# One row scale per chunk from norms, half-array products first, and first loads on two queues

## The chip, the cores and the metric

The kernel runs on one core of one Trainium2 chip. A core has five engines that run their own instruction lists in order and wait for each other by semaphores: TensorE (PE, with its weight loads shown as PEld), VectorE (DVE), ScalarE (ACT), GpSimd (POOL) and SyncE (SP), which here only issues DMAs. The metric is the device time of one execution in microseconds. Three timed runs of the kernel before took 1389.17, 1389.33 and 1389.57 us, so the median is 1389.33 us. All positions in time below are microseconds from the start of the span of the one profiled execution.

## What is computed

Cut to what matters, with B = 8, S = 4160, D = 192, H = 8 heads, K = 7 taps, and 33280 rows in all:

```
w   = softmax(weight_gen, axis=-1)              # per row and head, over 7 taps
y   = sum_k w[..., k, h] * x_pad[row + k]       # causal window of 7 rows of x
h   = y @ w_in                                  # 192 -> 1024
sm  = exp(h - max(h)) / (sum(exp(h - max(h))) + 1e-9)
s   = h * sm                                    # "solu"
ln  = (s - mean(s)) / sqrt(var(s) + 1e-6) * g_ln
out = ln @ w_out                                # 1024 -> 192
```

The output is normalised over each row of s, so a factor common to a row of s drops out again, except in the two small constants. The kernel uses this: it multiplies s by a scale of its own choice that keeps the 16-bit halves of s in range.

## The kernel before

The 33280 rows lie as 128 runs of 260 rows, one run on each partition, so a tile is one row of every run, 128 rows in all, and there are 260 tiles. x and weight_gen come in chunks: of 4 tiles, of 8, and then fifteen of 16. Per chunk, seven steps (t0 to t6) make the softmax over the taps on DVE, POOL and ACT. For each group of four tiles (two in the first chunk) POOL runs three tensor operations (line 133 multiplies x by the taps, lines 139 and 141 add), and DVE adds the last two parts (line 366, the step `fin`).

A tile then passes through these steps. PE transposes it (`xT`, line 383, two tiles at a time), ACT copies a rounded part (`xhi`, line 391), the rest comes from PE and ACT (`xn` and `xlo`, lines 398 and 405) or from DVE (`xld`, line 412). PE makes h (`mm1`): 192 rows of w_in are 128 and 64, the 128 use the whole array (line 422, six matmuls) and the 64 use one half of the array for each half of h (line 427, six matmuls, two at a time). DVE takes the negative maximum of the row (`max`, line 441). It then makes a bound out of the maximum (`vb`, line 445) and its reciprocal (`vr`, line 450), the scale of the row. ACT makes the exponentials (`exp`, line 454), DVE the product h times scale times exponential (`solu`, line 460), ACT the squares (`sq`, line 466) and a 16-bit part (`hi`, line 473), DVE the remaining 16-bit part (`lo`, line 477). One DMA transposes both (`tr`, line 485), PE makes the second product out of 24 matmuls (`mm2`, line 529), and ACT scales it (`out`, line 540). The factors of the rows come out of eight small steps per four tiles (f0 to f7, lines 497 to 516). A store follows per four tiles.

At the start w_in and w_out, which arrive as 64-bit floats, are turned into 32-bit floats by DVE and ACT out of integer pieces (lines 194 to 213), in seven parts. h lies in three PSUM buffers, so `mm1` of a tile waits for `sq` and `lo` of the tile three before. `po`, which `mm2` writes, has one buffer, so `mm2` waits for `out` of the tile before.

The order of the work on every engine is written out ahead: `issue_order` runs a list of steps with a cost, an earliest time and the steps each waits for, and picks on every engine the step with the lowest key, its tile number plus an entry of the table `URGENCY`. Nothing moves at run time. All DMAs stand on SP's queue. The loads of chunk 0 and the weights stand in the code ahead of that order: the first taps, two loads of the last 64 rows of w_in, then in `load_x(0)` a load of the six rows ahead of each run (line 78, 127 rows of the tile `xt`), of the first rows (line 79) and of zeros (line 80), and behind them the rest of w_in, w_out, g and chunk 1 (lines 168 to 177).

Of the kernel before, what the change touches and what calls it, by code (L numbers as in the profile page):

```python
# [26 lines left out]
def tile_kernel(ctx: ExitStack, tc: tile.TileContext, x, weight_gen, w_in, w_out, g_ln, out):  # L27
# [39 lines left out]
    def load_x(c, part=0):  # L67
# [5 lines left out]
        if c == 0:  # L73

            nc.gpsimd.memset(xt[:1, : HALO * D], 0.0)
            zeros = const.tile([B, D], F32, name="zeros")
            nc.gpsimd.memset(zeros, 0.0)
            nc.sync.dma_start(xv[1:, :HALO, :], x_run[: P - 1, RUN - HALO :, :])
            nc.sync.dma_start(xv[:, HALO : HALO + n, :], x_run[:, :n, :])
# [49 lines left out]

    def attention(xt, wt, t, n, half):  # L130
# [54 lines left out]
    def float_of_double(key, raw, n, step):  # L185
# [17 lines left out]
        elif step == 2:  # L203

            frac = big.tile([P, FF], F32, name="e")[:, :n]
# [18 lines left out]
    def last_rows(step):  # L224
        if step < 3:
            first["b"] = float_of_double("b", raw_b, FH, step)
        elif step == 3:
            nc.scalar.copy(wb_hi, first["b"])
        elif step == 4:
            nc.vector.tensor_tensor(  # L230
                out=wb_lo, in0=first["b"], in1=wb_hi.bitcast(F32), op=ALU.subtract
            )

# [26 lines left out]
    def scale_and_sum(f, step):  # L260
# [17 lines left out]
        elif step == 2:  # L278
            junk = big.tile([P, FF], F32, name="e")
# [5 lines left out]
    def prepare_second(step, half=None):  # L285
# [8 lines left out]
        elif step == 5:  # L294
            second["total"] = ps_a.tile([P, 512], F32, name="pa")
            nc.tensor.matmul(second["total"][:, :NP], ones, sq, start=True, stop=True)
# [119 lines left out]
    def first_product(t):  # L416
# [3 lines left out]
        for fs in halves:  # L420
            for n, (lhs, rhs) in enumerate(((hi, wa_hi), (hi, wa_lo), (lo, wa_hi))):
                nc.tensor.matmul(h[:, fs], lhs[:, 0, :], rhs[:, fs], start=n == 0, stop=False)  # L422

        for n, (lhs, rhs) in enumerate(((hi, wb_hi), (hi, wb_lo), (lo, wb_hi))):
            for f, fs in enumerate(halves):
                rows = slice(f * D2, (f + 1) * D2)
                nc.tensor.matmul(  # L427
                    h[:, fs], lhs[rows, 1, :], rhs[rows], start=False, stop=n == 2,
                )
# [12 lines left out]


    def bound(t):
        nc.vector.tensor_reduce(
            stat(t, BOUND), stat(t, NMAX, 2), axis=AX.X, op=ALU.max, apply_absolute_value=True
        )

    def row_scale(t):
        nc.vector.reciprocal(stat(t, SIGMA), stat(t, BOUND))  # L450
# [38 lines left out]
    def scales(t, step):  # L489
# [9 lines left out]
        if step == 0:  # L499
            nc.scalar.activation(of(ZE), of(Z), AF.Copy, bias=1e-9)  # L500
        elif step == 1:
            reduce(U, ZE, 2, ALU.mult)
        elif step == 2:
            nc.scalar.activation(of(E), of(U), AF.Square, scale=1e-3 * FF**1.5)
        elif step == 3:
            reduce(V, Q, 2, ALU.add)
        elif step == 4:
# [5 lines left out]
        elif step == 5:  # L513
            reduce(T, Y, 3, ALU.mult)
        elif step == 6:
# [3 lines left out]
        elif step == 7:  # L519
            reduce(OUT, Y2, 2, ALU.mult)  # L520
# [30 lines left out]
    def at_chunk(op, *args):  # L551
# [5 lines left out]
        max=maximum, vb=bound, vr=row_scale, exp=exponentials, solu=solu, sq=squares, hi=high_half, lo=low_half,  # L557
# [18 lines left out]
    for n in range(8):  # L576
        ops[f"f{n}"] = at(scales, n)
    for n in range(TAP_STEPS):
        ops[f"t{n}"] = at_chunk(softmax_taps, n)
# [9 lines left out]
    a00=-79.4, a01=-110.4, a02=-10.4, a03=-9.5, a04=28.3, a10=35.2, a11=8.2, a12=-10.4, a13=2,  # L589
    a14=-26.4, attA=14.7, attB=-118.7, b0=12.5, b1=28.4, b2=-7.8, b3=-40.9, b4=125.7, c00=120.1,  # L590
    c01=19.2, c02=4.8, c10=-143, c11=7.6, c12=1.7, c20=-15.4, c21=6.6, c22=-4.8, c30=-11.2,
    c31=-125.2, c32=78.7, dup=-17.9, exp=66.3, f0=73.9, f1=1.2, f2=-140.6, f3=-73.6, f4=-146.4,
    f5=-90.9, f6=-122.6, f7=-80.2, fin=-1.8, hi=21.6, lo=-147.6, lw=-22, lx0=-1.4, lx1=-11.2,
    lx2=-124.2, lx3=169.4, max=5.1, mm1=26.4, mm2=33.4, od=-130.9, out=-6, p30=-16.2, p31=3.9,
    p4=42.9, p5=103.1, p6=5.8, p70=-62.9, p71=0.3, p80=126.7, p81=-54.7, q00=-14.5, q01=-183.5,
    q02=-5.9, q10=-13.7, q11=-25.1, q12=-13.9, q20=-2.5, q21=-143.1, q22=-168.3, q30=-15.9,
# [246 lines left out]
```

## Time and profile before

| what | value |
|---|---|
| median of three timed runs | 1389.33 us |
| profiled execution, own time | 1389.4 us |
| its span | 1387.5 us, 1.9 us less than its time |
| mean granted PE clock | 0.991 |
| PE busy | 1259.2 us (91%) |
| POOL busy | 1247.0 us (90%) |
| DVE busy | 1230.0 us (89%) |
| ACT busy | 1128.5 us (81%) |
| first `max` (line 441) starts | 60.1 us |
| last `max` starts | 1365.3 us |

Busy time is the union of an engine's instructions, so operations that overlap on one engine are counted once. A group of instructions is named by line, engine, operation and the tiles it writes and reads, with its count, busy time and mean duration; behind the bar stands how long the engine was idle just ahead of them, and what ended that idle time. SPq is a DMA being issued on SP's queue; "issue" as releaser is time in which nothing in the profile was waited for.

### The profile page before, as it was taken

How to read it: one execution, taken by the hardware profiler on the slowest of the kernel's cores; microseconds unless marked ns; L12 is line 12 of the kernel's file. 1: busy time of each engine (PE TensorE's matmuls, PEld its weight loads, DVE VectorE, ACT ScalarE, POOL GpSimd, SP SyncE). 2: the span in 40 equal slices, each digit the busy share in tenths (PEclk: the TensorE clock that was granted, in tenths of full speed). 3: DMA queues.
4: the chain of work that ended last, by engine and by line, in shares of the span. 5: the costliest groups of instructions: out<-in, count | busy, mean ns of one | idle time of the engine just before them, and what ended most of it. 6: DMA issues, size and time to landing. Idle time of an engine off the chain costs nothing.

```text
span 1387.5 us, 26562 instructions
## 1 busy us (share of the span) xinstructions
PE 1259.2 (91%) x10028; PEld 988.6 (71%) x10028; DVE 1230.0 (89%) x2068; ACT 1128.5 (81%) x2231; POOL 1247.0 (90%) x243
## 2 busy tenths in 40 slices
PE   0389899999999999989989999999999999999997
PEld 0267677777777777767767677777777777777776
DVE  2999898999989899889989898989899889999984
ACT  1588887888888888888888888888788888888885
POOL 1999999999999999999999999999999999999100
PEclk9989999999999999999999999999999999999999
DMA  3469768696968789697857768687858668766765
GB/s 90 139 142 194 147 128 201 124 207 122 194 130 174 146 145 195 122 198 123 186 130 166 158 149 186 118 190 145 193 109 191 146 140 176 132 133 117 134 131 116
DMA packets 565241, 210.43 MB, mean 152 GB/s; under 512 B 544329, under 2 KB 545785, under 8 KB 565112
## 3 DMA queue, kind: packets, MB, share of 16 engines
q1 hardware_dynamic: 565112, 208.73, 72.5%
q8 instruction: 79, 1.29, 0.4%
q14 instruction: 50, 0.41, 0.1%
HBM read 46.19 MB, written 25.56 MB: 52 GB/s over the span
## 4 chain that ended last, share of the span: by engine, by line
POOL 51%; DVE 16%; issue 13%; ACT 13%; PE 4%; DMA 3%; SPq 0%; POOLq 0%; DVEq 0%; ACTq 0%
POOL pr L133 27%; POOL pr L139 15%; POOL half L141 6%; DVE h L460 5%; ACT hl L473 4%; DVE hl L477 4%; ACT e L466 3%; DVE stats L441 3%; ACT e L454 3%; DVE a L366 3%; DMA xt<-in_x_dram 2%; POOL wt L114 2%; PE po L529 2%; POOL wt L126 1%; PE h L422 1%
## 5 line engine op out<-in xcount | busy, mean ns | idle before, releaser
L133 POOL TENSOR_TENSOR pr<-xt,wt 128x5376 f32<-128x5376 f32 (+1 forms) x66 | 631.3, 9565 | 23.1 <-DMA xt<-zeros 20.5
L529 PE MATMUL po<-w_hl,hlT 128*128 128x192 f16 x6192 | 558.5, 247 | 26.6 <-ACT ot L540 26.2
L529 PEld LDWEIGHTS <-hlT 128*128 128x128 f16 x6240 | 515.2, 98 | 82.2 <-issue 79.2
L477 DVE SCALAR_TENSOR_TENSOR hl<-h,hl 128x1024 f16<-128x1024 f32 x260 | 315.4, 1220 | 44.2 <-ACT e L466 31.5
L460 DVE SCALAR_TENSOR_TENSOR h<-h,stats,e 128x1024 f32<-128x1024 f32 x260 | 334.7, 1288 | 22.4 <-ACT e L454 9.2
L473 ACT ACTIVATE hl<-h 128x1024 f16<-128x1024 f32 x260 | 267.3, 1028 | 92.3 <-DVE stats L497 57.4
L139 POOL TENSOR_TENSOR pr<-pr 128x2304 f32<-128x2304 f32 (+1 forms) x66 | 332.7, 5041 | 5.2
L441 DVE TENSOR_REDUCE stats<-h 128x1 f32<-128x1024 f32 x260 | 316.1, 1216 | 8.9 <-PE h L427 8.1
L454 ACT ACTIVATE e<-h,stats 128x1024 f32<-128x1024 f32 x260 | 292.6, 1126 | 31.1 <-DVE stats L441 27.2
L466 ACT ACTIVATE e<-h,stats 128x1024 f32<-128x1024 f32 x260 | 292.3, 1125 | 5.9 <-DVE hl L477 5.4
L422 PE MATMUL h<-wa_hi,x_hi 128*128 128x512 f32 x520 | 225.4, 433 | 36.3 <-ACT e L466 22.8
L141 POOL TENSOR_TENSOR half<-pr 128x1536 f32<-128x1536 f32 (+1 forms) x66 | 225.8, 3422 | 5.2
L422 PE MATMUL h<-wa_hi,x_lo 128*128 128x512 f32 x520 | 207.5, 399 | 0.8 <-ACT x_lo L405 0.8
L422 PE MATMUL h<-wa_lo,x_hi 128*128 128x512 f32 x520 | 206.3, 397 | 0.0
L422 PEld LDWEIGHTS h<-wa_hi,x_hi 128*128 128x128 f32 x520 | 98.9, 190 | 59.3 <-ACT e L466 26.0
L427 PE MATMUL h<-wb_hi,x_hi 64*128 64x512 f32 x520 | 131.1, 500 | 0.0
L383 PE MATMUL pa<-ident,a 128*128 128x128 f32 x520 | 84.6, 286 | 44.2 <-DVE a L366 44.1
L540 ACT ACTIVATE ot<-po,stats 128x192 f32<-128x192 f32 x258 | 111.4, 432 | 8.5 <-PE po L529 8.5
L366 DVE TENSOR_REDUCE a<-half 128x768 f32<-128x1536 f32 (+1 forms) x66 | 116.4, 1764 | 1.6 <-POOL half L141 1.6
L427 PEld LDWEIGHTS h<-wb_hi,x_hi 64*128 64x128 f32 x520 | 48.6, 184 | 96.7 <-issue 96.7
L422 PEld LDWEIGHTS h<-wa_hi,x_lo 128*128 128x128 f32 x520 | 98.6, 190 | 24.3 <-ACT x_lo L405 1.6
L383 PEld LDWEIGHTS pa<-ident,a 128*128 128x128 f32 x520 | 55.8, 142 | 79.7 <-DVE a L366 44.1
(79 smaller groups left out, 1194.1 us busy)
## 6 DMA issues: line engine op xcount, KB each, us to landing
out_dram<-ot SPq DMA_DIRECT2D x65, 384.0 KB, 3.3
xt<-in_x_dram SPq DMA_DIRECT2D x30, 576.0 KB, 4.7
xt<-in_x_dram SPq DMA_DIRECT2D x30, 480.0 KB, 4.7
wt<-in_weight_gen_dram SPq DMA_DIRECT2D x15, 448.0 KB, 4.1
hlT<-hl SPq DMA_TRANSPOSE x260, 4.5
raw<-in_moe_w_out_dram SPq DMA_DIRECT2D x1, 1536.0 KB, 9.4
xt<-in_x_dram SPq DMA_DIRECT2D x3, 384.0 KB, 6.0
raw_a<-in_moe_w_in_dram SPq DMA_DIRECT2D x2, 512.0 KB, 11.5
```

The source lines that it names most:

```text
L133: nc.gpsimd.tensor_tensor(out=window(pr, 0, [(TG * D, K), (HG, n * H), (1, HG)]), in0=window(xt, t * D, [(D, K), (HG, n * H), (1, HG)]), i ...
L139: nc.gpsimd.tensor_tensor(out=pr[:, :3], in0=pr[:, :3], in1=pr[:, 3:6], op=ALU.add)
L141: nc.gpsimd.tensor_tensor(out=half, in0=window(pr, 0, [(2 * TG * D, 2), (D, n), (1, D)]), in1=window(pr, TG * D, [(5 * TG * D, 2), (D, n), ...
L422: nc.tensor.matmul(h[:, fs], lhs[:, 0, :], rhs[:, fs], start=n == 0, stop=False)
L427: nc.tensor.matmul(h[:, fs], lhs[rows, 1, :], rhs[rows], start=False, stop=n == 2,)
L441: nc.vector.tensor_reduce(stat(t, NMAX), h_of[t], axis=AX.X, op=ALU.max, negate=True)
L454: nc.scalar.activation(e, h_of[t], AF.Exp, bias=stat(t, NMAX), accum_out=stat(t, Z))
L460: nc.vector.scalar_tensor_tensor(out=h, in0=h, scalar=stat(t, SIGMA), in1=e, op0=ALU.mult, op1=ALU.mult, accum_out=stat(t, M))
L466: nc.scalar.activation(e_of.pop(t), h_of[t], AF.Square, bias=stat(t, M), scale=-float(FF), accum_out=stat(t, Q),)
L473: nc.scalar.activation(hl[:, 0, :], h_of[t], AF.Copy, scale=2.0**14)
L477: nc.vector.scalar_tensor_tensor(out=hl[:, 1, :], in0=h_of[t], scalar=2.0**14, in1=hl[:, 0, :], op0=ALU.mult, op1=ALU.subtract,)
L529: nc.tensor.matmul(po[:, :D], hlT[:, half * NJ + j, :], w2_hl[:, j, w, :], start=n == 0, stop=n == len(terms) - 1,)
```

## The change

Four things change.

First, the scale of a row of s is no longer made out of its maximum. One number per partition and chunk is made from the norm of the rows of x in the chunk (and of the chunk before) times the norm of the columns of w_in: ACT squares x with a sum (`v00` to `v03`, four pieces for a chunk of 16), DVE adds the sums (`v1`), ACT takes the root by a logarithm and an exponential (`v2`) and multiplies by the norm of w_in (`v3`), DVE takes the reciprocal (`v4`), and ACT makes two constants for the factors (`v5`). The norm of w_in comes once, at the start, from three maxima on DVE, a square on ACT, a matmul and a sum (`n0` to `n6`). The steps `vb` and `vr` of each tile go, and two of the eight small steps per four tiles.

Second, `mm1` does its six half-array matmuls first and its six whole-array matmuls after them.

Third, the first loads are issued on SP and on ACT. The six rows ahead of each run come in eight loads of 15 rows, four on each queue, onto a tile that POOL has set to zero; x of chunk 0 comes ahead of w_in; 128 rows of w_in, half of w_out and g are on ACT's queue.

Fourth, the planner's costs, earliest times and the table `URGENCY` change, and with them the order on every engine.

The diff, cut to its core:

```diff
-            nc.gpsimd.memset(xt[:1, : HALO * D], 0.0)
-            zeros = const.tile([B, D], F32, name="zeros")
-            nc.gpsimd.memset(zeros, 0.0)
-            nc.sync.dma_start(xv[1:, :HALO, :], x_run[: P - 1, RUN - HALO :, :])
+            nc.gpsimd.memset(xt[:, : HALO * D], 0.0)
             nc.sync.dma_start(xv[:, HALO : HALO + n, :], x_run[:, :n, :])
-            nc.sync.dma_start(
-                xv[::PB, :HALO, :], zeros.unsqueeze(1).broadcast_to([B, HALO, D])
-            )
+            for b in range(B):
+                queue = nc.sync if b % 2 else nc.scalar
+                queue.dma_start(
+                    xv[b * PB + 1 : (b + 1) * PB, :HALO, :],
+                    x_run[b * PB : (b + 1) * PB - 1, RUN - HALO :, :],
+                )
...
+    def norm_x(c, step, part=0):
+        n = starts[c + 1] - starts[c]
+        if step == 0:
...
+            nc.scalar.activation(
+                junk[:, : (r1 - r0) * D].rearrange("p (t d) -> p t d", d=D), xv[:, r0:r1, :],
+                AF.Square, accum_out=squares_x[:, c + 1, part : part + 1],
+            )
+        elif step == 1:
+            row_of[c] = small.tile([P, 7], F32, name="row", bufs=5)
+            nc.vector.tensor_reduce(
+                row_of[c][:, SUM], squares_x[:, c : c + 2], axis=AX.XY, op=ALU.add
+            )
+        elif step == 2:
+            row = row_of[c]
+            nc.scalar.activation(row[:, LN], row[:, SUM], AF.Ln, bias=floor)
+            nc.scalar.activation(row[:, NORM], row[:, LN], AF.Exp, scale=0.5)
+        elif step == 3:
+            row = row_of[c]
+            nc.scalar.activation(row[:, LIMIT], row[:, NORM], AF.Copy, bias=0.5, scale=column)
+        elif step == 4:
+            nc.vector.reciprocal(row_of[c][:, SCALE], row_of[c][:, LIMIT])
...
+    load_x(0)
+    raw_a = att.tile([P, 2 * FF], I32, name="raw_a", bufs=1)
     raw_b = big.tile([P, FF], I32, name="hl", bufs=3)
     for f in range(2):
+        nc.scalar.dma_start(raw_a[:, f * FF : (f + 1) * FF], w_in[:P, f * FF : (f + 1) * FF])
         nc.sync.dma_start(raw_b[f * D2 : (f + 1) * D2, :], w_in[P:, f * FF : (f + 1) * FF])
-    load_x(0)
+    load_w(1)
...
+        (nc.scalar if n else nc.sync).dma_start(
+            raw_2v[:, js], w_out.rearrange("(j p) d -> p j d", p=P)[:, js]
+        )
+    g = const.tile([P, NJ], F32, name="g")
+    nc.scalar.dma_start(g, g_ln.rearrange("(j p) -> p j", p=P))
+    load_x(1)
...
+    def norm_of_first(step):
+        if step < 3:
+            nc.vector.tensor_reduce(
+                sq[:, 4 + step : 5 + step], first["b" if step == 2 else step], axis=AX.X,
+                op=ALU.max, apply_absolute_value=True,
+            )
...
-        for fs in halves:
-            for n, (lhs, rhs) in enumerate(((hi, wa_hi), (hi, wa_lo), (lo, wa_hi))):
-                nc.tensor.matmul(h[:, fs], lhs[:, 0, :], rhs[:, fs], start=n == 0, stop=False)
 
         for n, (lhs, rhs) in enumerate(((hi, wb_hi), (hi, wb_lo), (lo, wb_hi))):
             for f, fs in enumerate(halves):
                 rows = slice(f * D2, (f + 1) * D2)
-                nc.tensor.matmul(
-                    h[:, fs], lhs[rows, 1, :], rhs[rows], start=False, stop=n == 2,
-                )
+                nc.tensor.matmul(h[:, fs], lhs[rows, 1, :], rhs[rows], start=n == 0, stop=False)
+        for fs in halves:
+            for n, (lhs, rhs) in enumerate(((hi, wa_hi), (hi, wa_lo), (lo, wa_hi))):
+                nc.tensor.matmul(h[:, fs], lhs[:, 0, :], rhs[:, fs], start=False, stop=n == 2)
         h_of[t] = h
...
-    def bound(t):
-        nc.vector.tensor_reduce(
-            stat(t, BOUND), stat(t, NMAX, 2), axis=AX.X, op=ALU.max, apply_absolute_value=True
-        )
-
-    def row_scale(t):
-        nc.vector.reciprocal(stat(t, SIGMA), stat(t, BOUND))
...
-            out=h, in0=h, scalar=stat(t, SIGMA), in1=e, op0=ALU.mult, op1=ALU.mult, accum_out=stat(t, M)
+            out=h, in0=h, scalar=row(t, SCALE), in1=e, op0=ALU.mult, op1=ALU.mult, accum_out=stat(t, M)
...
-            nc.scalar.activation(of(ZE), of(Z), AF.Copy, bias=1e-9)
+            nc.scalar.activation(of(E), of(Z), AF.Square, bias=row(t, EPS_Z), scale=row(t, EPS))
         elif step == 1:
-            reduce(U, ZE, 2, ALU.mult)
-        elif step == 2:
-            nc.scalar.activation(of(E), of(U), AF.Square, scale=1e-3 * FF**1.5)
-        elif step == 3:
             reduce(V, Q, 2, ALU.add)
...
-    a00=-79.4, a01=-110.4, a02=-10.4, a03=-9.5, a04=28.3, a10=35.2, a11=8.2, a12=-10.4, a13=2,
+    a00=70.4, a01=-67.8, a02=-0.5, a03=-22.6, a04=-5.9, a10=-33.8, a11=58.9, a12=5, a13=-106.8,
...
-        add("attA", t, POOL, 14206 if full else 7302, *after, ready=21100 if c == 1 else 0)
+        add("attA", t, POOL, 14990 if full else 7500, *after, ready=15000 if c == 1 else 9000)
...
-        add("mm1", t, PE, 2300, low_of(t), ("sq", t - 3), ("lo", t - 3), *after)
+        add("mm1", t, PE, 2400, low_of(t), ("sq", t - 3), ("lo", t - 3), *after)
```

What the new costs and the new table do to the program is an order of rows on each engine. Three places follow, before and after.

At the start of the program on ACT, before (L201 and L202 are conversions of w_in, L118 and L122 steps of the taps' softmax):

```order
L56 ACT_TABLE_LOAD
L201 ACTIVATE h<-h 128x512
L202 ACTIVATE h<-h 128x512
L118 ACTIVATE wt<-wt 128x224
L122 ACTIVATE wy<-wm 128x32
```

The same place after the change (L145 squares x with a sum, L248 and L249 are the conversions, L306 a rounded copy of w_in):

```order
L56 ACT_TABLE_LOAD
L79 DMA xt<-in_x_dram 15x1152 x4
L195 DMA raw_a<-in_moe_w_in_dram 128x1024 x2
L202 DMA raw_101<-in_moe_w_out_dram 128x4x384
L206 DMA g<-in_moe_g_ln_dram 128x8x1
L118 ACTIVATE wt<-wt 128x224
L145 ACTIVATE junk,squares_x<-xt 128x1920
L122 ACTIVATE wy<-wm 128x32
L248 ACTIVATE h<-h 128x512
L249 ACTIVATE h<-h 128x512
```

Eight DMA issues now stand ahead of ACT's first computation, and the squares of x stand ahead of the copy L122 on which the first taps rest.

On DVE in the middle of the program, before (L441 maximum, L445 and L450 bound and reciprocal, L460 solu, L477 low half, L366 attention's last sum, L497 small steps):

```order
L460 SCALAR_TENSOR_TENSOR h,stats<-h,stats,e 128x1024
L441 TENSOR_REDUCE stats<-h 128x1
L445 TENSOR_REDUCE stats<-stats 128x1
L450 RECIPROCAL stats<-stats 128x1
L477 SCALAR_TENSOR_TENSOR hl<-h,hl 128x1024
L366 TENSOR_REDUCE a<-half 128x4x192
L460 SCALAR_TENSOR_TENSOR h,stats<-h,stats,e 128x1024
```

And after, where the same steps are L505, L515, L532 and L433, and L479 is `xld`:

```order
L515 SCALAR_TENSOR_TENSOR h,stats<-h,row,e 128x1024
L505 TENSOR_REDUCE stats<-h 128x1
L532 SCALAR_TENSOR_TENSOR hl<-h,hl 128x1024
L515 SCALAR_TENSOR_TENSOR h,stats<-h,row,e 128x1024
L505 TENSOR_REDUCE stats<-h 128x1
L479 TENSOR_TENSOR x_lo<-pa,x_hi 128x512
L532 SCALAR_TENSOR_TENSOR hl<-h,hl 128x1024
L515 SCALAR_TENSOR_TENSOR h,stats<-h,row,e 128x1024
L433 TENSOR_REDUCE a<-half 128x4x192
```

The two small rows per tile are gone. What moves besides is how far attention stands ahead of the maxima. Counted in the order of DVE, the row of attention's last sum for tiles 100 to 103 stands behind the maximum of tile 94 before and of tile 97 after, that for tiles 224 to 227 behind tile 212 before and 219 after, and the last one, for tiles 256 to 259, behind tile 244 before and 250 after.

On PE one tile's first product, before, with its neighbour behind it (L529 is the second product):

```order
L422 MATMUL h<-wa_hi,x_lo 128x512
L427 MATMUL h<-wb_hi,x_hi 128x512 x2
L427 MATMUL h<-wb_lo,x_hi 128x512 x2
L427 MATMUL h<-wb_hi,x_lo 128x512 x2
L383 MATMUL pa<-ident,a 128x128 x4
```

And after (L491 half arrays, L494 whole array):

```order
L491 MATMUL h<-wb_hi,x_hi 128x512 x2
L491 MATMUL h<-wb_lo,x_hi 128x512 x2
L491 MATMUL h<-wb_hi,x_lo 128x512 x2
L494 MATMUL h<-wa_hi,x_hi 128x512
L494 MATMUL h<-wa_lo,x_hi 128x512
L494 MATMUL h<-wa_hi,x_lo 128x512
```

The array is still switched twice per tile, into halves and back. The matmul that follows the switch back is now the first whole-array one of the same tile, where it was a matmul of another product.

More of the change, by code (lines that the diff above doesn't have):

```diff
@@ L232, in last_rows @@
             )
+    def norm_of_first(step):
[4 more added lines that the diff above has]
+            )
+        elif step == 3:
+            nc.scalar.activation(sq[:, 4:7], sq[:, 4:7], AF.Square)
+        elif step == 4:
+            first["total"] = ps_o.tile([P, 512], F32, name="po")
+            nc.tensor.matmul(first["total"][:, :3], ones, sq[:, 4:7], start=True, stop=True)
+        elif step == 5:
+            nc.vector.tensor_reduce(
+                first["total"][:, 8:9], first["total"][:, :3], axis=AX.X, op=ALU.add
+            )
+        elif step == 6:
+            nc.scalar.activation(column, first["total"][:, 8:9], AF.Ln, scale=1.05 * FF)
+            nc.scalar.activation(column, column, AF.Exp, scale=0.5)
     def first_rows(f, step):
@@ L294, in prepare_second @@
         elif step == 5:
-            second["total"] = ps_a.tile([P, 512], F32, name="pa")
-            nc.tensor.matmul(second["total"][:, :NP], ones, sq, start=True, stop=True)
+            second["total"] = second["sums"][:, 256:]
+            nc.tensor.matmul(second["total"][:, :NP], ones, sq[:, :NP], start=True, stop=True)
         elif step == 6:
@@ L556, in tile_kernel @@
         xhi=high_x, xn=subtract_high, xlo=low_x, xld=low_x_on_vector, mm1=first_product,
-        max=maximum, vb=bound, vr=row_scale, exp=exponentials, solu=solu, sq=squares, hi=high_half, lo=low_half,
+        max=maximum, exp=exponentials, solu=solu, sq=squares, hi=high_half, lo=low_half,
         tr=transpose_s, mm2=second_product, out=finish, od=store, lw=at_chunk(load_w),
@@ L575, in tile_kernel @@
         ops[f"lx{n}"] = at_chunk(load_x, n)
-    for n in range(8):
+    for n in range(6):
         ops[f"f{n}"] = at(scales, n)
+    for n in range(7):
+        ops[f"n{n}"] = once(norm_of_first, n)
+    for n in range(1, 6):
+        ops[f"v{n}"] = at_chunk(norm_x, n)
+    for part in range(4):
+        ops[f"v0{part}"] = at_chunk(norm_x, 0, part)
     for n in range(TAP_STEPS):
@@ L645, in issue_order @@
     once("p4", ACT, 660, "p6")
+    once("n3", ACT, 100, "n0", "n1", "n2")
+    once("n4", PE, 220, "n3")
+    once("n5", DVE, 70, "n4")
+    once("n6", ACT, 400, "n5")
     for half in "01":
@@ L664, in issue_order @@
             add("lw", t, SP, 1270, last_group(c - 3))
-            add("lx0", t, SP, 1540, last_group(c - 2))
+            add("lx0", t, SP, 1540, last_group(c - 2), *parts_of(c - 2))
             for n in range(1, loads):
                 add(f"lx{n}", t, SP, 1540, (f"lx{n - 1}", t))
+        whole = starts[c + 1] - t == 16
+        for part in range(4 if whole else 1):
+            size = 830 if whole else 1800
+            if c > 1:
+                load = min(part + 1, loads - 1) if whole else loads - 1
+                add(f"v0{part}", t, ACT, size, (f"lx{load}", t))
+            else:
+                add(f"v0{part}", t, ACT, size, ready=15000)
+        add_norms(c, t)
         n = (starts[c + 1] - t) * 8
@@ L670, in issue_order @@
         wide = 60 + 7.3 * n
-        costs = (wide, 13 * n, 190 + 6 * n, wide, 190 + n, 60 + 8.4 * n, 13 * n)
+        costs = (wide, 13.5 * n, 100 + 6 * n, wide, 100 + n, 60 + 6.3 * n, 13.5 * n)
         for k in range(7):
```

131 lines of the change are left out of this document (74 added, 57 removed).

## The prediction

> **What bounds the kernel now.** I read the page first, then the windows of busy time, the rows of single lines, the waits, and the timeline of the start. A difference of 0.2% (2.8 us) is what a measurement of this kernel can tell from none.
>
> ```profile
> span 1387.5 us, 26562 instructions
> PE 1259.2 (91%) x10028; PEld 988.6 (71%) x10028; DVE 1230.0 (89%) x2068; ACT 1128.5 (81%) x2231; POOL 1247.0 (90%) x243
> ```
>
> Three engines are near full, so shares decide nothing; stages do. The windows give PE, PEld, DVE, ACT and POOL busy in each stretch.
>
> ```profile
> 300.00:400.00 100.00, 95.11 (x768) 74.68 (x765) 91.47 (x151) 84.68 (x166) 99.06 (x19) 1.00 0.81 166
> 1290.00:1340.00 50.00, 49.32 (x396) 38.50 (x395) 44.27 (x78) 42.34 (x86) 0.00 (x0) 1.00 0.65 122
> ```
>
> In the middle POOL is full, at 99.06 of 100. Behind 1290 it has nothing left, yet 98 us follow. How the tiles lie in this, the windows of the maximum (line 441, one per tile) and of attention's last sum (line 366, one per four tiles, two per four in chunk 0) tell, and the row of line 441 with its first and last start:
>
> ```profile
> L441 DVE TENSOR_REDUCE stats<-h x260: 1186/1216/1230, 60.1 to 1365.3; 128x1 f32<-128x1024 f32 x130
> 0.00:100.00 100.00, 9.11 (x8) 0.95 0.44 122
> 100.00:1290.00 1190.00, 287.45 (x237) 1.00 0.76 157
> 0.00:100.00 100.00, 5.49 (x4) 0.95 0.44 122
> 100.00:1290.00 1190.00, 109.16 (x61) 1.00 0.76 157
> 1290.00:1388.00 98.00, 19.49 (x16) 0.98 0.64 122
> ```
>
> The second and third rows are line 441, the next two line 366, the last line 441 again. Maxima run at (1365.3 - 60.1)/259 = 5.04 us per tile. At 100 us attention is at tile 12 (2 x 2 + 2 x 4) and the maximum at 8; in the next 1190 us attention makes 61 x 4 = 244 tiles, 4.88 us each, the maximum 237. So the lead of attention grows, and 16 maxima remain when POOL is done. The front part shows the same growth in the order: attention's sum stands 6 tiles ahead of the maximum at tile 100 and 12 at tile 256. Does POOL merely outrun the others, or does it hold them? The waits between 100 and 1290:
>
> ```profile
> ACT hl L473 <- DVE stats L497: 48.6, 58, 1.6
> ACT wt L118 <- POOL wt L114: 37.1, 13, 4.5
> PE po L529 <- ACT ot L540: 21.1, 22, 3.1
> PE h L422 <- ACT e L466: 13.7, 11, 4.3
> PE h L422 <- DVE hl L477: 9.3, 12, 1.5
> PE pa L398 <- ACT x_hi L391: 9.2, 15, 2.4
> ```
>
> Once per chunk ACT, in its fixed order, stands 37.1/13 = 2.9 us until POOL has subtracted the taps' maximum (line 114); exponentials, squares and copies queue behind it, and PE then waits for ACT. POOL holds the others there, and in an order whose lead grows, tiles come out slower than POOL makes them. POOL's own pace:
>
> ```profile
> L133 POOL TENSOR_TENSOR pr<-xt,wt x66: 4942/9708/9735, 31.6 to 1270.0; 128x5376 f32<-128x5376 f32 x64, 128x2688 f32<-128x2688 f32 x2
> 1284.98 3.48 POOL L141 TENSOR_TENSOR half<-pr 128x1536 f32<-128x1536 f32 x1
> ```
>
> From 31.6 to 1288.5 is 1256.9 us, 4.83 us per tile. PE's pace: a tile has 10028/260 = 38.6 matmuls, so 300:400 held 768/38.6 = 19.9 tiles at 95.11/19.9 = 4.78 us of PE each. PE's four waits above sum to 53.3 us over 237 tiles, 0.22 per tile: 4.78 + 0.22 = 5.00, near the measured 1190/237 = 5.02.
>
> **The start.** The timeline of the first 32 us, and the chain's first piece:
>
> ```profile
> 2.46 26.27 DMA xt<-in_x_dram
> 2.46 0.48 SPq L78 DMA_DIRECT2D xt<-in_x_dram  x1
> 2.99 9.88 SPq L79 DMA_DIRECT2D xt<-in_x_dram  x1
> 31.08 0.69 DVE L194 TENSOR_SCALAR h<-raw_a 128x512 int32<-128x512 int32 x1 [20.61 <-DMA raw_a<-in_moe_w_in_dram]
> 31.59 4.95 POOL L133 TENSOR_TENSOR pr<-xt,wt 128x2688 f32<-128x2688 f32 x1 [20.46 <-DMA xt<-zeros]
> xt<-in_x_dram SPq DMA_DIRECT2D x1, 571.5 KB
> xt<-zeros SPq DMA_DIRECT2D x1, 36.0 KB
> hl<-in_moe_w_in_dram SPq DMA_DIRECT2D x2, 256.0 KB, 3.6
> raw<-in_moe_w_out_dram SPq DMA_DIRECT2D x1, 1536.0 KB, 9.4
> 28.82 2.62 DMA xt<-zeros
> ```
>
> The load of 127 rows needs 26.27 us for 571.5 KB, 22 KB/us; w_out on 128 rows made 163 KB/us. The zeros wait for it and all later issues queue behind them, so POOL and DVE stand idle 20 us each. The change removes this load. How wide 15 rows go no row shows. Bounds: as narrow as the 127, 15/127 x 26.27 = 3.1 us each and 24.8 for eight in a row; or like the other loads, 2.6 us (8 rows) to 3.6 us (64 rows), side by side. I take the second, which is nearer in size and shape, and keep the first as a rival.
>
> The Trainium skill, "DMA: Bandwidth & Descriptors", section "Why a DMA increments its semaphore by 16 and not by 1", lets a transfer use the largest number of engines up to 16 that divides its slowest dimension: 127 rows give one engine, 15 rows give 15. The 22 KB/us agrees for 127; by this rule the eight loads land in a few us, which is the value taken. The same page, "Issuing engines are not separate DMA queues", says that a second queue saves issue time alone: by that, four halo issues of some 0.5 us, 2 us, are all that ACT's queue gives here.
>
> Now the sum. Ahead of the first attention come taps (112 KB), x (384) and halos (540): 1036 KB at 163 KB/us, 6.4 us, so x is there at about 8. ACT then squares 1920 columns ahead of the taps' next step. Its price, with the other added and removed work:
>
> ```profile
> L280 ACT ACTIVATE e<-raw_a 128x384 f32<-128x384 f32 x4 | 2.1, 524 | 0.1
> L466 ACT ACTIVATE e<-h,stats 128x1024 f32<-128x1024 f32 x260 | 292.3, 1125 | 5.9 <-DVE hl L477 5.4
> L466 ACT ACTIVATION_READ_ACCUMULATOR e<-h,stats 128x1 f32 x260 | 56.0, 215 | 0.0
> L445 DVE TENSOR_REDUCE stats<-stats 128x1 f32<-128x2 f32 x260 | 38.2, 147 | 1.4
> L450 DVE RECIPROCAL stats<-stats 128x1 f32<-128x1 f32 x260 | 41.4, 159 | 5.1
> L500 ACT ACTIVATE stats<-stats 128x4 f32<-128x4 f32 x63 | 15.2, 241 | 0.4
> ```
>
> By line 280 and 466 a column costs (1125 - 524)/640 = 0.94 ns: 1920 columns take 2.0 us and the read 0.2. DVE's next step of the taps stands behind five conversions of w_in (0.7 us each, 3.5); w_in's first 512 KB end 512/163 = 3 us after x, at 11. So the taps go on at 14.6, and with 2 us for their last steps on ACT, DVE and POOL, attention starts at **16.5** instead of 31.6. DVE converts from 31.1 to the first maximum at 60.1, 29.0 us. Now it begins at 11 and has the first part of w_in (three of 0.7), three norm maxima (about 0.65, half of line 441's 1.216) and some small rows more: 33.9 us, and I add 2, since ACT squares chunk 1 (1536 columns) ahead of the last conversions and so waits for that load. First maximum at **47**, bounds 44 (no such wait) and 52 (768 KB of chunk 1 late by 5 us): 13 us earlier.
>
> **Per tile.** DVE loses lines 445 and 450, 0.31 us (0.15, if half of each lies under its neighbour). ACT gains four squares of 768 columns per 16 tiles, 0.89 + 0.2 each: 0.27 per tile, five small rows per chunk (0.08), less one small row per four tiles (0.06): +0.29, on 4.34 (1128.5/260). DVE falls from 4.73 to about 4.4. Neither is then the longest; POOL stays at 4.83. PE's price for the other order:
>
> ```profile
> 705.92 0.40 PE L422 MATMUL h<-wa_lo,x_hi 128*128 128x512 f32 x1
> 706.15 0.40 PE L422 MATMUL h<-wa_hi,x_lo 128*128 128x512 f32 x1
> 706.48 0.50 PE L427 MATMUL h<-wb_hi,x_hi 64*128 64x512 f32 x2
> 706.82 0.39 PE L427 MATMUL h<-wb_lo,x_hi 64*128 64x512 f32 x2
> 707.05 0.40 PE L427 MATMUL h<-wb_hi,x_lo 64*128 64x512 f32 x2
> 707.38 2.15 PE L529 MATMUL po<-w_hl,hlT 128*128 128x192 f16 x24
> ```
>
> Starts lie 0.23 apart. Into the halves they lie 0.33 and 0.34 apart, 0.21 lost; back to the second product 0.33 once, 0.10 lost. Now the matmul behind the switch back is a 512-column one, and I price that switch as the way in, 0.21: 0.42 instead of 0.31, +0.1 where PE did not wait anyway. Bounds: -0.1 (always after a wait, so that the way in is free) and +0.1. I take +0.1, since only 11 + 12 of 237 tiles waited for their buffer: PE 4.88.
>
> "TensorEngine Tiling (Array Packing)" of the Trainium skill, section "Tiling Modes", has it that changing the mode drains the array. By that alone two changes per tile cost the same in either order, +0.0, and the pace would be POOL's (the case of 1322 below); the rows agree on the drain but show unequal prices.
>
> Waits: PE's 0.22 fall. POOL's costs in the planner rise, and the order now holds attention a steady 4 to 6 tiles ahead, so ACT need not stand at the taps; I leave 0.04. That makes **4.92** per tile. If these waits were covered by other late work, they would come back at 0.22.
>
> **Sum** of the profiled execution: 47 + 259 x 4.92 + (1387.5 - 1365.3) + 1.9 outside the span = 1345. By POOL's side: 16.5 + 1256.9 = 1273, then not 16 but some 10 maxima, 10 x 4.88, and 22.2 + 1.9: 1346. The profiled execution took 1389.4, the median 1389.33. **Forecast 1345 us**, its own range 1333 to 1358.
>
> **Rivals.** *POOL's pace alone* (0.14): the half-array order costs nothing and no wait is left, 4.83 per tile: 47 + 1251 + 24 = 1322. For it: POOL at 99.06 of 100. Against: PE at 4.78 has no room.
>
> *Only the start* (0.13): the others are the slower ones, the lead was POOL outrunning them, and ACT's new work eats what DVE gains: 5.04 per tile, 47 + 1305 + 24 = 1376. For it: PE's 95 of 100; against: ACT's 37 us behind POOL.
>
> *The 15 rows stay on one engine* (0.05), so this part does not do what it says: x at 27, attention at 31 as before, and with 10 maxima after POOL 31 + 1257 + 49 + 24 = 1361.
>
> *ACT becomes the bound* (0.06), the slower side: the chain of one tile runs solu, hi, sq, exp, solu, with ACT in three of the links, so ACT's waits (48.6 us behind DVE alone) stay and its 0.29 comes on top: 5.33 per tile, 47 + 1380 + 24 = 1451. It decides slower from a pace of 5.09, where 259 x 0.05 eats the 13 us. For it: ACT's squares stand in order ahead of exponentials and wait for loads of x. Against: DVE gives back 0.31 on just that chain.
>
> **Chances and range.** Forecast 0.60, POOL's pace 0.14, only the start 0.13, narrow halos 0.05, ACT 0.06, and 0.02 for no difference. Faster 0.60 + 0.14 + 0.13 + 0.05 = 0.92, same 0.02, slower 0.06. The range runs from POOL's pace to only the start, 1322 to 1376; it leaves out ACT's case and the outer edges, with first maximum at 44 or 52 (3 or 5 us).
>
> **What would show it.** Start: POOL's first row of attention near 16.5, first maximum near 47, no DMA piece of 26 us in the chain. Pace: maxima 4.92 us apart, about 10 of them behind POOL's last row instead of 16. PE: both kinds of weight load in a tile idle ahead of a switch, with 0.33 to 0.34 between starts at both. ACT: its wait for line 114 per chunk gone, busy above 4.6 per tile. The forecast is wrong if maxima stay 5.0 apart, or if ACT waits for loads of x in each chunk.

## The result and the profile after

The changed kernel takes 1375.47 us (median of four runs, 1373.68 to 1378.33), the kernel before 1389.25 us in the same comparison. The ratio is 0.9902, with a 95% interval of 0.9881 to 0.9923: 13.8 us faster, where 44 were forecast. The profiled execution took 1377.17 us, its span is 1375.4 us. The page of the changed kernel, and the rows of the maximum (now line 505) and of attention's first operation (now line 174) with their first and last starts:

```profile
span 1375.4 us, 26071 instructions
PE 1265.9 (92%) x10030; PEld 1001.1 (73%) x10030; DVE 1180.8 (86%) x1523; ACT 1192.3 (87%) x2383; POOL 1246.9 (91%) x241
L505 DVE TENSOR_REDUCE stats<-h x260: 1158/1218/1229, 47.5 to 1356.5; 128x1 f32<-128x1024 f32 x130
L174 POOL TENSOR_TENSOR pr<-xt,wt x66: 4943/9707/9728, 17.3 to 1285.8; 128x5376 f32<-128x5376 f32 x64, 128x2688 f32<-128x2688 f32 x2
```

The start came out as forecast, 17.3 and 47.5 us (16.5 and 47). The pace did not: maxima lie (1356.5 - 47.5)/259 = 5.05 us apart, as they did before (5.04), although DVE has lost 49 us of work. POOL's last row and the window behind it, in which the maxima are counted:

```profile
1300.82 3.47 POOL L182 TENSOR_TENSOR half<-pr 128x1536 f32<-128x1536 f32 x1
1304.30:1375.00 70.70, 14.65 (x12) 1.00 0.68 133
```

POOL ends at 1304.3 with 12 maxima still to come. From its first row of attention at 17.3 it needs 1287.0 us, 30 more than the 1256.9 of before, although its busy time is the same (1246.9 and 1247.0).

The start in the timeline of the changed kernel, with the landing times of the loads of 15 rows behind it:

```profile
1.82 3.59 SPq L79 DMA_DIRECT2D xt<-in_x_dram  x4
1.82 1.91 ACTq L79 DMA_DIRECT2D xt<-in_x_dram  x4
8.68 1.79 ACT L145 ACTIVATE junk<-xt 128x1920 f32<-128x1920 f32 x1
11.98 0.69 DVE L241 TENSOR_SCALAR h<-raw_a 128x512 int32<-128x512 int32 x1 [8.58 <-DMA raw_a<-in_moe_w_in_dram]
17.32 4.94 POOL L174 TENSOR_TENSOR pr<-xt,wt 128x2688 f32<-128x2688 f32 x1
xt<-in_x_dram SPq DMA_DIRECT2D x4, 67.5 KB, 3.8
xt<-in_x_dram ACTq DMA_DIRECT2D x4, 67.5 KB, 4.2
```

The loads of 15 rows land some 4 us after their issue (medians 3.8 and 4.2), and the eight overlap. The piece of 26 us is gone.

The waits of the changed kernel between 100 and 1290 us, longest ones of ACT first, then of POOL and PE:

```profile
ACT hl L528 <- DVE h L515: 44.2, 48, 1.1
ACT junk L145 <- DMA xt<-in_x_dram: 37.1, 19, 3.4
POOL wt L126 <- DVE wy L124: 26.5, 8, 4.2
PE po L580 <- ACT ot L591: 21.0, 18, 2.1
PE pa L465 <- ACT x_hi L458: 16.6, 11, 2.5
```

ACT's wait for the taps (37.1 us before) is no longer among the long ones. In its place stands one of the same size to the tenth: the squares of x (line 145) wait 37.1 us for loads of x. PE waits for ACT as before. POOL, which has no wait in this window before, now stands 26.5 us until DVE has the reciprocal of the taps' sum (line 124), and 3.5 us more ahead of the same line 126: 30.0 us, the length by which its work stretched. One of ACT's waits for x in the timeline, first on SP's queue, then on ACT:

```profile
841.22 2.94 SPq L540 DMA_TRANSPOSE hlT<-hl  x1
844.21 0.57 SPq L90 DMA_DIRECT2D xt<-in_x_dram  x1
```

```profile
845.21 1.12 ACT L509 ACTIVATE e<-h,stats 128x1024 f32<-128x1024 f32 x1
846.55 0.22 ACT L561 ACTIVATE stats<-stats 128x8 f32<-128x8 f32 x1
848.63 0.84 ACT L145 ACTIVATE junk<-xt 128x768 f32<-128x768 f32 x1 [1.86 <-DMA xt<-in_x_dram]
849.47 0.38 ACT L567 ACTIVATE stats<-stats,newton 128x4 f32<-128x4 f32 x1
849.75 0.56 ACT L458 CAST x_hi<-pa 128x512 fp32r<-128x512 f32 x1
```

The load of x is issued at 844.21, behind the transposing DMA that has held SP's queue since 841.22. The square that needs it stands next in ACT's order at 846.77 and starts at 848.63. A factor step and the copy `xhi`, on which PE waits, stand behind it.

The two switches per tile on PE:

```profile
902.32 0.50 PE L491 MATMUL h<-wb_hi,x_hi 64*128 64x512 f32 x2
902.66 0.39 PE L491 MATMUL h<-wb_lo,x_hi 64*128 64x512 f32 x2
902.89 0.40 PE L491 MATMUL h<-wb_hi,x_lo 64*128 64x512 f32 x2
903.21 0.50 PE L494 MATMUL h<-wa_hi,x_hi 128*128 128x512 f32 x1
903.55 0.40 PE L494 MATMUL h<-wa_lo,x_hi 128*128 128x512 f32 x1
903.78 0.39 PE L494 MATMUL h<-wa_hi,x_lo 128*128 128x512 f32 x1
```

Starts lie 0.34 us apart behind the way in, and 0.32 and 0.34 on the way back, where 0.23 is the normal step. The way back loses 0.20 us, as it was priced (0.21).

### The profile page after: what moved, and what is told of

Read it like the earlier page. It is cut to its first block, busy times and chain, and to the rows that moved or that the text cites. A ratio compares the mean times of both kernels' runs of the same rounds, so it can differ in the third digit from the quotient of the medians.

```text
span 1375.4 us, 26071 instructions
## 1 busy us (share of the span) xinstructions
PE 1265.9 (92%) x10030; PEld 1001.1 (73%) x10030; DVE 1180.8 (86%) x1523; ACT 1192.3 (87%) x2383; POOL 1246.9 (91%) x241
## 5 line engine op out<-in xcount | busy, mean ns | idle before, releaser
L532 DVE SCALAR_TENSOR_TENSOR hl<-h,hl 128x1024 f16<-128x1024 f32 x260 | 315.9, 1218 | 75.1 <-ACT e L521 57.1
L515 DVE SCALAR_TENSOR_TENSOR h<-h,row,e 128x1024 f32<-128x1024 f32 x260 | 333.8, 1286 | 21.4 <-ACT e L509 18.2
L505 DVE TENSOR_REDUCE stats<-h 128x1 f32<-128x1024 f32 x260 | 316.6, 1218 | 25.6 <-PE h L494 24.5
L494 PE MATMUL h<-wa_hi,x_hi 128*128 128x512 f32 x520 | 233.8, 450 | 0.0
L494 PE MATMUL h<-wa_lo,x_hi 128*128 128x512 f32 x520 | 206.6, 397 | 0.0
L494 PE MATMUL h<-wa_hi,x_lo 128*128 128x512 f32 x520 | 206.2, 397 | 0.0
L494 PEld LDWEIGHTS h<-wa_hi,x_hi 128*128 128x128 f32 x520 | 98.1, 189 | 107.4 <-issue 95.7
L491 PE MATMUL h<-wb_hi,x_hi 64*128 64x512 f32 x520 | 130.9, 500 | 16.0 <-DVE w_hl L390 7.4
L433 DVE TENSOR_REDUCE a<-half 128x768 f32<-128x1536 f32 (+1 forms) x66 | 116.3, 1762 | 0.0
L450 PE MATMUL pa<-ident,a 128*128 128x128 f32 x520 | 80.8, 278 | 37.8 <-DVE a L433 31.7
L494 PEld LDWEIGHTS h<-wa_hi,x_lo 128*128 128x128 f32 x520 | 98.5, 189 | 23.1
L494 PEld LDWEIGHTS h<-wa_lo,x_hi 128*128 128x128 f32 x520 | 98.9, 190 | 11.9
L491 PE MATMUL h<-wb_hi,x_lo 64*128 64x512 f32 x520 | 104.0, 396 | 0.0
```

The lines of the kernel that those rows point to most:

```text
L491: nc.tensor.matmul(h[:, fs], lhs[rows, 1, :], rhs[rows], start=n == 0, stop=False)
L494: nc.tensor.matmul(h[:, fs], lhs[:, 0, :], rhs[:, fs], start=False, stop=n == 2)
L505: nc.vector.tensor_reduce(stat(t, NMAX), h_of[t], axis=AX.X, op=ALU.max, negate=True)
L515: nc.vector.scalar_tensor_tensor(out=h, in0=h, scalar=row(t, SCALE), in1=e, op0=ALU.mult, op1=ALU.mult, accum_out=stat(t, M))
L532: nc.vector.scalar_tensor_tensor(out=hl[:, 1, :], in0=h_of[t], scalar=2.0**14, in1=hl[:, 0, :], op0=ALU.mult, op1=ALU.subtract,)
```

## Experiments

All ratios are to the kernel before, timed beside each. Two theories stand against each other at first. Theory PE: PE sets the pace, with the dearer order of the matmuls and waits that stay. Theory ACT: ACT, in its fixed order, stands for loads of x, and everything in the loop of a tile stands with it.

**Whole-array matmuls first again in the changed kernel.**

```diff
-        for n, (lhs, rhs) in enumerate(((hi, wb_hi), (hi, wb_lo), (lo, wb_hi))):
-            ...
-        for fs in halves:
-            ...
+        for fs in halves:
+            for n, (lhs, rhs) in enumerate(((hi, wa_hi), (hi, wa_lo), (lo, wa_hi))):
+                nc.tensor.matmul(h[:, fs], lhs[:, 0, :], rhs[:, fs], start=n == 0, stop=False)
+        for n, (lhs, rhs) in enumerate(((hi, wb_hi), (hi, wb_lo), (lo, wb_hi))):
+            ...
```

> The changed kernel with the whole-array matmuls first in a tile again, all else and the order of instructions between tiles as changed. Theory PE (PE sets the pace, its busy time of 4.82 to 4.88 us per tile plus waits that stay): PE gets back about 0.1 us per tile, so 15 to 26 us less, 1350 to 1360 us. Theory ACT (the pace is set by ACT standing in order for loads of x and for DVE): PE waits longer by what it saves, within 5 us of 1375.

Measured: 1371.65 us, ratio 0.9877 (0.9862 to 0.9892). That is 3.8 us below the changed kernel, with intervals that overlap. Theory PE falls: 15 to 26 us should have come back.

**Half-array matmuls first in the kernel before.** The same edit the other way round.

> The kernel before with the half-array matmuls first in a tile, nothing else. If PE sets the pace before as well: 15 to 26 us more, 1404 to 1415 us. If POOL holds the kernel before, as the prediction had it: PE's longer tiles go into its waits, within 5 us of 1389.

Measured: 1389.83 us, ratio 1.0004 (0.9995 to 1.0014). PE's busy time between 100 and 1290 us rises from 1131.56 to 1143.77 us, and no time is lost. PE did not set the pace of the kernel before.

**The new first loads alone in the kernel before.**

```diff
-            nc.sync.dma_start(xv[1:, :HALO, :], x_run[: P - 1, RUN - HALO :, :])
             nc.sync.dma_start(xv[:, HALO : HALO + n, :], x_run[:, :n, :])
-            nc.sync.dma_start(
-                xv[::PB, :HALO, :], zeros.unsqueeze(1).broadcast_to([B, HALO, D])
-            )
+            for b in range(B):
+                queue = nc.sync if b % 2 else nc.scalar
+                queue.dma_start(...)
...
+    load_x(0)
...
```

The loads of w_in, w_out and g stand behind it as in the changed kernel.

> The kernel before with the new first loads alone (eight loads of 15 rows, two queues, x ahead of w_in). No squares stand on ACT, so attention and conversions start at about 14 and the first maximum near 43 to 46 instead of 60. If all of this reaches the end: 1373 to 1377 us. If the order ties tiles to something later than the start, less than half of it arrives: 1383 or more.

Measured: 1374.14 us, ratio 0.9896 (0.9879 to 0.9912): 14.6 us, about all of what the whole change brings. Attention starts at 16.5, later than the 14 expected. The first maximum starts at 44.7 us and the last at 1350.3, 5.04 us apart, and ACT's wait for the taps stays:

```profile
L441 DVE TENSOR_REDUCE stats<-h x260: 1201/1217/1231, 44.7 to 1350.3; 128x1 f32<-128x1024 f32 x130
ACT wt L118 <- POOL wt L114: 34.7, 12, 4.6
```

So the start is worth what was forecast, and the other parts of the change together give nothing or cancel.

**No squares of x in the chunks of 16.**

```diff
+            if n != TC:
                 nc.scalar.activation(..., AF.Square, accum_out=squares_x[:, c + 1, part : part + 1])
...
     nc.vector.memset(squares_x, 0.0)
+    nc.vector.memset(squares_x[:, 4:], 7.7)
```

> The changed kernel without the squares of x on ACT in the fifteen chunks of 16 (the sums are a constant, so the row scale is not made from x there; the rest of the steps stays). Theory ACT: the 37 us of waits for loads of x and 60 x 1.0 us of work go from ACT, and the pace falls by 0.1 to 0.2 us per tile, 1325 to 1350 us. Theory PE: only PE's waits for ACT shrink, 5 to 15 us less, 1360 to 1370 us.

Measured: 1338.29 us, ratio 0.9636 (0.9621 to 0.9650). The squares cost 37 us. (There is one more chunk of 8 than said above: 4 + 8 + 8 + 15 x 16 = 260 tiles. So 60 of the 63 squares stand in the chunks of 16.) Maxima lie (1318.9 - 49.4)/259 = 4.90 us apart:

```profile
L507 DVE TENSOR_REDUCE stats<-h x260: 1161/1219/1233, 49.4 to 1318.9; 128x1 f32<-128x1024 f32 x130
```

**The same squares of something that is always there.** This tells the work from the wait.

```diff
+            src = wa_hi.bitcast(F32)[:, : 4 * D].rearrange("p (t d) -> p t d", d=D)
             nc.scalar.activation(
                 junk[:, : (r1 - r0) * D].rearrange("p (t d) -> p t d", d=D),
-                xv[:, r0:r1, :],
+                src if n == TC else xv[:, r0:r1, :],
```

> The changed kernel whose squares in the chunks of 16 read w_in's rounded columns, which never change, instead of x: the same instructions on ACT, but no wait for a load, and the row scale there is not made from x. If it is ACT's waits for loads of x (37 us in 19 waits) that cost the 37 us between the changed kernel and the one without squares: near 1340 us. If it is ACT's added work (about 60 x 1.0 us): near 1372. Between them, each has its share.

Measured: 1340.12 us, ratio 0.9652 (0.9637 to 0.9666). With all of the work and none of the waits the time is within 2 us of that without the squares. ACT is busy 1090.35 us between 100 and 1290 there, against 1060.85 in the changed kernel, because more tiles pass in that window (244 maxima against 236). No instruction waits for these squares in the changed kernel but two weight loads, 0.3 us in all, so a late square delays what stands behind it on ACT. The cost was the wait. The maxima and POOL's longest wait:

```profile
L507 DVE TENSOR_REDUCE stats<-h x260: 1202/1218/1226, 48.4 to 1321.3; 128x1 f32<-128x1024 f32 x130
POOL wt L126 <- DVE stats L554: 1.5, 1, 1.5
```

POOL's 30.0 us of waits have shrunk to 1.5, so they came from ACT's wait as well: POOL needs the taps' last steps, and one of them (line 122) stands in ACT's order.

**The kernel before with a constant scale.**

```diff
     def bound(t):
-        nc.vector.tensor_reduce(stat(t, BOUND), ...)
+        pass
     def row_scale(t):
-        nc.vector.reciprocal(stat(t, SIGMA), stat(t, BOUND))
+        pass
...
-    nc.gpsimd.memset(stats[:, :, :, HALF], 0.5)
+    nc.gpsimd.memset(stats[:, :, :, SIGMA], 2.0)
```

> The kernel before without the bound and the reciprocal of each tile (lines 445 and 450; the scale is the constant 2.0, which the bound gives for these inputs wherever no value of h is above 0.5). If DVE's 0.31 us per tile matter to the pace of the kernel before: up to 0.1 to 0.2 us per tile, 1340 to 1365 us. If the kernel before is held by POOL and its order: 1385 to 1389.

Measured: 1386.24 us, ratio 0.9981 (0.9971 to 0.9990). DVE's busy time between 100 and 1290 falls by 41.7 us (1090.78 to 1049.10), and 2.4 us arrive. The rest became idle time of DVE. ACT's wait for POOL grew by 9.9 us, from 37.1:

```profile
ACT wt L118 <- POOL wt L114: 47.0, 13, 4.9
```

**Late squares.** A version that keeps the whole computation: the planner may place the squares of a chunk only behind the exponentials of the tiles 18 to 12 ahead of it. They are needed at the chunk's first `solu`, so there is room.

```diff
-                add(f"v0{part}", t, ACT, size, (f"lx{load}", t))
+                add(f"v0{part}", t, ACT, size, (f"lx{load}", t), ("exp", t - 18 + 2 * part))
```

> The changed kernel with the squares of a chunk of 16 held back in the planner until the exponentials of the tiles 18, 16, 14 and 12 ahead of the chunk, so that the loads of x have landed; the planner orders all engines anew. Theory that the waits for x cost: the waits go and the time falls to 1340 to 1355 us. Theory that the work costs: 1368 to 1378.

Measured: 1342.43 us, ratio 0.9667 (0.9652 to 0.9681), 33 us below the changed kernel; with the next version, 0.3 us from it, it is the fastest of all that compute everything. Line 145 no longer appears among ACT's waits. Its maxima and attention:

```profile
L505 DVE TENSOR_REDUCE stats<-h x260: 1160/1218/1235, 48.0 to 1320.6; 128x1 f32<-128x1024 f32 x130
L174 POOL TENSOR_TENSOR pr<-xt,wt x66: 4940/9711/9750, 17.8 to 1258.3; 128x5376 f32<-128x5376 f32 x64, 128x2688 f32<-128x2688 f32 x2
1276.70:1341.00 64.30, 12.21 (x10) 1.00 0.66 129
```

The third row is the window behind POOL's last row: ten maxima remain. Maxima lie (1320.6 - 48.0)/259 = 4.91 us apart. The planner orders all engines anew here, so this run alone does not show that the wait was the cause; with the squares of a constant, whose order is the changed kernel's, it does.

**Late squares with whole-array matmuls first.** Both edits together.

> The same late squares with the whole-array matmuls first in a tile again. If waits for x held the pace and PE is next, PE's 0.05 to 0.1 us per tile now count in full: 10 to 25 us below the late squares alone. If ACT still sets the pace: within 5 us of it, as between the changed kernel and its whole-array-first form (3.8 us).

Measured: 1342.71 us, ratio 0.9667 (0.9653 to 0.9682). Nothing, although PE's busy time between 100 and 1290 is 10.5 us less (1157.45 to 1167.91). PE's order is not on the path there either.

**POOL's real costs in the planner of the kernel before,** with the new first loads.

```diff
-        add("attA", t, POOL, 14206 if full else 7302, ...)
-        add("attB", t, POOL, 3380 if full else 1764, ...)
+        add("attA", t, POOL, 14990 if full else 7500, ...)
+        add("attB", t, POOL, 3510 if full else 1800, ...)
...
-        costs = (wide, 13 * n, 190 + 6 * n, wide, 190 + n, 60 + 8.4 * n, 13 * n)
+        costs = (wide, 13.5 * n, 190 + 6 * n, wide, 190 + n, 60 + 8.4 * n, 13.5 * n)
```

> The kernel before with the new first loads (1374.1 us) and with POOL's costs in the planner raised to the changed kernel's: attention now stands a steady 3 to 4 tiles ahead of the maxima in the order, where the lead grew to 12. If POOL and a growing lead hold the kernel before, as the prediction had it: ACT's waits for the taps (34.7 us) go, POOL's pace reaches the end, 1335 to 1350 us. If PE, DVE and ACT set the pace of the kernel before: 1368 to 1378.

Measured: 1348.44 us, ratio 0.9703 (0.9689 to 0.9718), 25.7 us below the first loads alone, with the old scale and the old order of matmuls. ACT's wait for the taps shrinks from 34.7 us:

```profile
ACT wt L118 <- POOL wt L114: 2.5, 1, 2.5
L441 DVE TENSOR_REDUCE stats<-h x260: 1197/1216/1259, 45.1 to 1325.0; 128x1 f32<-128x1024 f32 x130
```

This agrees with the reading that the growing lead of attention in the order held the kernel before, through the taps on ACT; since the whole order is new, it is not a proof of it.

**Costlier loads of x in the planner of the changed kernel.**

```diff
-            add("lx0", t, SP, 1540, last_group(c - 2), *parts_of(c - 2))
+            add("lx0", t, SP, 3600, last_group(c - 2), *parts_of(c - 2))
             for n in range(1, loads):
-                add(f"lx{n}", t, SP, 1540, (f"lx{n - 1}", t))
+                add(f"lx{n}", t, SP, 3600, (f"lx{n - 1}", t))
```

> The changed kernel with one planner cost raised: a load of x takes 3600 ns of transfer instead of 1540, so the planner sets the squares of a piece one to four tiles later. If ACT's waits come from the planner's too early landing of x: most of the 37 us of waits go, 1340 to 1355 us. If the late squares were faster for another reason of their new order: 1365 or more.

Measured: 1345.88 us, ratio 0.9684 (0.9670 to 0.9698). One wait of 0.9 us for x is left between 100 and 1290. This agrees with the reading that the planner counted on loads that land too early: by its own terms (450 + 650 + 1540 + 950 ns) a load of x lands 3.6 us after its issue if nothing else is in flight, and in the trace of the changed kernel it takes 4.5 in the median, 2.7 to 7.6. The order of all engines is new here too.

**Only the fourth square per chunk of a constant.** As above, with `part == 3` added to the condition.

> The changed kernel whose fourth square per chunk of 16 (and that one alone) reads w_in's rounded columns instead of x; order and work unchanged, the row scale not made from x in that piece. By the trace of the changed kernel about half of the wait stands at the first square of a chunk and half at the fourth. If each microsecond that ACT stands for x costs one at the end: half of the 35 us goes, 1353 to 1362. If one wait in a chunk is as bad as two: within 6 us of 1375.

Measured: 1362.50 us, ratio 0.9806 (0.9791 to 0.9820). The time lies 0.5 us above the expected 1353 to 1362: the fourth square held 38% of the wait, not half. ACT's waits for x fall from 37.1 to 23.1 us, and the time by 13.0:

```profile
ACT junk L146 <- DMA xt<-in_x_dram: 23.1, 12, 3.4
```

14.0 us less of this wait, 13.0 us less time; all 37.1 us of it, 35.4 us less time (1375.47 to 1340.12). Each microsecond of it costs nearly one, to within the 4 or 5 us that such runs differ among themselves. POOL's waits go the same way: 30.0 us in the changed kernel, 17.1 here, 1.5 with all squares of a constant.

**The new first loads on one queue.** In the kernel before with the new loads, every `nc.scalar.dma_start` of the start becomes `nc.sync.dma_start`.

> The kernel before with the new first loads, all issued on SP's queue, none on ACT's. If the gain of the first loads is that of the 127 rows and of the sequence: within 4 us of the 1374.1 us with two queues (eight issues of some 0.5 us stand in row). If two queues carry more than one: 1380 or more.

Measured: 1376.41 us, ratio 0.9908 (0.9891 to 0.9924), 2.3 us above two queues, with intervals that overlap. Attention even starts at 8.0 us here, because no DMA issue stands ahead of the taps on ACT:

```profile
8.05 4.95 POOL L133 TENSOR_TENSOR pr<-xt,wt 128x2688 f32<-128x2688 f32 x1 [2.04 <-DMA xt<-in_x_dram]
16.14 0.69 DVE L194 TENSOR_SCALAR h<-hl 128x512 int32<-128x512 int32 x1 [10.78 <-DMA hl<-in_moe_w_in_dram]
L441 DVE TENSOR_REDUCE stats<-h x260: 1195/1215/1235, 47.3 to 1352.3; 128x1 f32<-128x1024 f32 x130
```

That brings nothing: the conversions of w_in on DVE start at 16.14 instead of 13.17 with two queues, and the first maximum at 47.3 instead of 44.7. What the start is worth is read from the first maximum, not from attention.

## Why the prediction was wrong

The median, 1375.47, lies just inside the range, at its upper end, but the forecast of 1345 was wrong by 30 us: the gain is 14 us and not 44. The case that came out is the rival "only the start" by its number, though not by its reasons. Both things that the prediction named as showing it wrong came: maxima stayed 5.05 us apart, and ACT waited for loads of x.

**The start: right.** Attention at 17.3 (16.5), DVE's conversions at 11.98 (11), the first maximum at 47.5 (47). The loads of 15 rows landed in 4 us. The Trainium skill's rule in "DMA: Bandwidth & Descriptors", section "Why a DMA increments its semaphore by 16 and not by 1", by which 127 rows go to one engine and 15 rows to 15, agrees with this: 540 KB in eight such loads were in within 8.7 us, where one engine at the rate of the 127 rows needs 24.8. The Trainium skill's section "Issuing engines are not separate DMA queues" on the same page, by which a second issuing engine saves issue time alone, agrees too: 2.3 us between one queue and two, not clear of noise. The issues on ACT have a price, since they stand ahead of ACT's own work: the taps' first step on ACT (line 118) starts at 8.90 with two queues and at 3.90 with one.

**DVE's and ACT's work: about right in size.** DVE's busy time fell by 49 us, to 4.54 us per tile where about 4.4 was forecast; ACT's busy time came to 1192.3/260 = 4.59 us per tile (4.63). That DVE would not set the pace was right: 41.7 us taken from it moved the kernel before by 2.4. That ACT would not was right for its work (1340.12 us with the squares of a constant, 1338.29 without squares) and wrong for its waits.

**PE's price: twice too large, and worth nothing in time.** PE's busy time rose by 0.05 us per tile (1137.78/236 against 1131.56/237), where 0.1 was forecast. In three pairs (1.0004 in the kernel before; 3.8 us with overlapping intervals in the changed one; 0.3 us with late squares) the order of the matmuls moved the time by nothing that can be told. The forecast counted it as 26 us on the path. The Trainium skill's "TensorEngine Tiling (Array Packing)", section "Tiling Modes", says only that a change of the mode drains the array; the equal price in either order that the prediction drew from it is off by these 0.05 us in busy time, and in time no run here tells the two prices apart.

**The failed step: "I leave 0.04"**, the last term of the pace. PE's waits of 0.22 us per tile were said to fall because ACT need not stand at the taps any more. It does not stand there any more, but PE's waits stayed: PE's five longest sum to 50.8 us (the two shown above, and 4.6, 4.6 and 4.0) over 236 tiles, 0.22 again, because ACT now stands 37.1 us for loads of x. The square of a piece was costed as work on ACT (1.1 us, 0.27 per tile), and its wait was not costed at all, except inside the rival "ACT becomes the bound", which named that squares wait for loads of x and gave it no price. Part of it could have been seen ahead: by the profile of before a load of x lands 4.7 us after its issue, a microsecond more than the planner's 3.6. The trace of the changed kernel shows the rest: in the place shown above the load stands behind a transpose that holds SP's queue 2.94 us, and its square's turn on ACT comes 2.6 us after the issue. The second sum, by POOL's side, fails with the same step: it took POOL's 1256.9 us as given, and POOL needed 1287.0, because its taps wait for ACT too.

**What its other terms were worth.** With that wait gone and nothing else changed, the changed kernel takes 1340.12 us, with late squares 1342.43, and in both the maxima come 4.91 us apart; with late squares ten of them lie behind POOL's last row. These are near the forecast's 1345, 4.92 and "some 10", but in part by luck: with the squares of a constant PE is busy 1164.53/244 = 4.77 us per tile and waits 0.10 (24.8 us), where the forecast had 4.88 and 0.04. What sets the pace once the wait is gone stays open. POOL works almost without a wait there (1.2 us between 100 and 1290; line 174 starts first at 17.8 and last at 1258.3 in the kernel with late squares), but they did so before as well (31.6 to 1270.0) with 16 maxima left behind them; PE's order and ACT's squares make no difference, and no run here shortens POOL's work.

**What held the kernel before: right as far as shown.** Taking POOL's true costs into its planner removed ACT's wait at the taps and 25.7 us. The new order of the changed kernel does not hold attention at a steady distance, as the prediction had it: by the front part's own count the lead is 3 tiles at tile 100 and 6 at the end, where it was 6 and 12. So of the change, the loads brought 14.6 us; the rest of it gained about 34 us and lost 35 again, since ACT's wait for the taps went and one for x of the same size took its place (1374.14 us with the loads alone, 1340.12 without the wait for x, 1375.47 with it). What the new scale itself is worth stays open: the kernel before with the true costs has 1348.44 us without it, the changed kernel with late squares 1342.43 with it, and the two differ in their whole order.

## What to carry to other kernels

When an in-order engine gets an instruction that depends on a DMA, cost its wait and not only its duration: take the landing time from the profile, add what stands ahead of the load on its queue, and see what is queued behind the waiting instruction. An engine that is 87% busy can still set the pace, if it stands in the loop of a tile: here each microsecond ACT stood for a load cost nearly one at the end, while 42 us of work taken from DVE in the kernel before and 10 from PE in the one with late squares gave 2 and nothing. In this kernel a planner's cost that was too low, for POOL or for a load of x, went with about one wait of ACT per chunk at the place where the orders meet (13 and 19 waits in 15 chunks); the runs with that cost raised were 25.7 and 29.6 us faster, with a new order on every engine.

## What was not expected of the hardware

A transposing DMA holds SP's queue for about 2 us, from 1.3 to 4.6, before the next issue; the loads of x from chunk 2 on hold it 0.57 us in the median, up to 1.5. At the start single plain loads hold it longer too, 9.88 us before the change. The transposes stand in the way of loads that share the queue:

```profile
L540 SPq DMA_TRANSPOSE hlT<-hl x260: 1317/1955/4552, 55.8 to 1364.6; - x130
```

And the factors g, 4 KB in pieces of 4 bytes, took 15.7 us to land, with other loads in flight (9.1 in the kernel before):

```profile
g<-in_moe_g_ln_dram ACTq DMA_DIRECT2D x1, 4.0 KB, 15.7
```
